# The first loads of an attention and spectral-mixing kernel: another queue for w_phi, another place for one weight load

## The chip, the cores and the metric

The kernel runs on one core of one Trainium2 chip. The metric is device time in microseconds (us), the median of the runs; the kernel before has 440.7 us in three runs (440.68 to 441.16). A core has five engines with an instruction stream each: TensorE (PE, matrix products; PEld is its loading of weights), VectorE (DVE), ScalarE (ACT), GpSimd (POOL) and SyncE (SP). Loads and stores are issued from one of these streams and carried out by 16 DMA engines that all issuers share. In the profile q0 is the DMA queue of what GpSimd issues, and q1 holds what SyncE issues.

## What is computed

The reference is an attention with a feature map, followed by a mixing of frequencies and channels:

```python
def phi(x):
    proj = einsum('bhsd,df->bhsf', x, w_phi)
    proj = proj - max(abs(proj), axis=-1)
    return concatenate([exp(proj), exp(-proj)], axis=-1)
q_p, k_p = phi(q), phi(k)
kv, z = einsum('bhsf,bhsd->bhfd', k_p, v), sum(k_p, axis=2)
x = einsum('bhsf,bhfd->bhsd', q_p, kv) / (einsum('bhsf,bhf->bhs', q_p, z) + 1e-6)
# heads side by side: x is (8, 576, 512)
X = rfft(x, axis=1)
Y[:, :64] = (Xr w_r - Xi w_i) + 1j (Xr w_i + Xi w_r)      # one matrix per mode
u = x + irfft(Y)
out = u + maximum(u @ w_ch, 0)
```

q, k and v are (8, 8, 576, 64) in float32, w_phi is 64 x 128. w_r and w_i are 64 matrices of 512 x 512 each, 134 MB together in float32, by far the most of what is read.

## The kernel before

The attention is cut into 16 units (class Unit, L101): a unit is two heads (g, 0 to 3) by two batches (bp, 0 to 3). Each unit loads its part of k and q as bfloat16 (load_k L105, load_q L109; the load converts) and of v as float32 (load_v L113). Each of these is one DMA with 2 x 128 rows of 2304 bytes on the reading side. The loop at L503 runs the units as a pipeline: in step n, one unit has its k and q turned by TensorE (turn_k, turn_q), the next earlier one gets its features and exponentials (rows_k, exp_k, rows_q), and the one before has its kv product, numerator and transform (weigh_v2, kv, num, freq). weigh_v2 multiplies v into va; that is the first use of a unit's v.

The weights w_r and w_i come in 64 loads of 1 MB as they land (2 MB as they are read), eight modes of 128 channels each; wload (L340) issues one, always on GpSimd, which converts float32 to bfloat16. next_w(n) (L359) issues the next n in the fixed list wq. The first of them, (0, 0), lands in the space of yacc (home, L327), the second in that of XT. Nine buffers of a pool and a few lent spaces hold the weights; mix (L461) uses them up, in the loop of the units through some (L488), and after it in the loop at L923, together with the second part: product with w_ch, inverse transform, relu, stores (Channels, Absorb, Last).

Each engine runs its instructions in the order of the program (class InOrder, L27): a helper records every instruction, and so the profile gives most of them the line L37. The tiles' names tell them apart. An instruction that waits for a semaphore holds up all that stands behind it in its engine's stream, the issues of DMAs among it.

The change is in the prologue, L365 to L386. There SyncE issues v of the first unit, w_phi twice (once for each half of the partitions, into scr, a space lent by xs) and v of the second unit (L368 to L371). GpSimd issues k and q of the first unit (L372, L373), then computes index tables with five kinds of iota (si, pi, nine, mi, L374 to L383) and the identity matrix (make_identity, L385), and then issues the first weights (next_w(1), L386); k and q of the second unit and another weight load come at L497 to L499. ScalarE begins with the loading of its function table for the sine, and then computes the sine (csf, L420). VectorE turns si and mi into angles (L400 to L419), casts the identity to ident_b (L421), which TensorE needs for every transpose, and casts w_phi into the two blocks of w2blk (L423, L424), which the first products of rows_k need.

Of the kernel before, what the change touches and what calls it, by code (L numbers as in the profile page):

```python
# [43 lines left out]
def kernel(  # L44
# [14 lines left out]
    pe, dve, act = (InOrder(tc, e) for e in (nc.tensor, nc.vector, nc.scalar))  # L59
    pool, sp = InOrder(tc, nc.gpsimd), InOrder(tc, nc.sync)  # L60
# [279 lines left out]
    def wload(g, w):  # L340
        wt = home(g, w)
        o, i = w // 2, w % 2
        w = (moe_w_r, moe_w_i)[i]
        pool.dma_start(
            wt.rearrange("p m r e -> p m (r e)"),
            w[MG * o:MG * o + MG, g * 128:(g + 1) * 128, :].rearrange(
                "m (p r) e -> p m (r e)", r=2))
        return wt
# [10 lines left out]
    def next_w(n):  # L359
        for _ in range(n):  # L360
            if wq:
                key = wq.pop(0)
                wts[key] = wload(*key)

    scr = xs[:, 1].rearrange("p b n d -> p (b n d)").bitcast(F32)  # L365
    wpf = scr[:, 1920:2048]
    units = [Unit(g, bp) for g in range(NG) for bp in range(NP)]
    units[0].load_v(sp)  # L368
    sp.dma_start(wpf[0:64, :], w_phi)
    sp.dma_start(wpf[64:128, :], w_phi)  # L370
    units[1].load_v(sp)  # L371
    units[0].load_k()  # L372
    units[0].load_q()  # L373
    si = const.tile([128, 5], I32, name="si")  # L374
    pool.iota(si[0:64, 0:4], [[1, 4]], base=0, channel_multiplier=9)
    pool.iota(si[0:64, 4:5], [[1, 1]], base=8, channel_multiplier=9)
# [6 lines left out]
    pool.iota(mi, [[4, 2], [8, NO], [1, 4]], base=0, channel_multiplier=0)  # L383
    ident_f = scr[:, 2176:2304]
    make_identity(nc, ident_f)  # L385
    next_w(1)  # L386

    w2blk = const.tile([128, 256], BF16, name="w2blk")
    wchb = const.tile([128, 4, 512], BF16, name="wchb")
# [664 lines left out]
```

## Time and profile before

| | before |
|---|---|
| median of 3 runs (lowest to highest) | 440.7 us (440.68 to 441.16) |
| span of the profiled execution, first to last instruction | 440.0 us |
| mean granted clock of TensorE | 0.909 |
| TensorE, matrix products busy | 326.7 us (74%) |
| VectorE busy | 296.0 us (67%) |
| ScalarE busy | 279.1 us (63%) |
| GpSimd busy | 112.5 us (26%) |
| read from HBM, written to it | 163.64 MB, 9.44 MB |

The profile is of one execution, whose time from end to end is not among the three runs; what it gives is the span, 0.7 us under their median. A busy time is the sum over the span and says nothing of where an engine was late. The page has the span in 40 slices of 11 us with the busy tenths of each engine and of the DMA engines, then the DMA queues with their share of 16 engines, then the chain of work that ended last, and the costliest groups of instructions with the idle time ahead of them. The trace behind it can be asked for one stretch of time: which instruction began when, what it waited for, and how many packets and bytes each queue moved. The DMA share can go over 1, since packets of one engine overlap. MB and GB/s of the page count the bytes that land.

### The profile page before, as it was taken

The page shows a single profiled execution, that of the slowest core. Times are in us where ns is not written, and L with a number is a line of the kernel's source. Part 1 is how long each engine was busy: PE and PEld are TensorE (multiplying, and loading weights), DVE is VectorE, ACT ScalarE, POOL GpSimd, SP SyncE. Part 2 cuts the span into 40 slices and gives each one's busy share as a digit, 9 for nine tenths or more (in the row PEclk, how much of TensorE's full clock was granted, in tenths as well). Part 3 has the DMA queues.
Part 4 walks back from the last instruction along what each step waited for, and adds up shares of the span by engine and source line. Part 5 has one row for each costly group of instructions (what it writes and reads, how often), then busy time and mean ns, then how long its engine had stood idle before and what let it go on. Part 6 is the DMA issues. An engine that isn't in the chain of part 4 may idle for free.

```text
span 440.0 us, 10106 instructions
## 1 busy us (share of the span) xinstructions
PE 326.7 (74%) x4190; PEld 199.7 (45%) x4233; DVE 296.0 (67%) x583; ACT 279.1 (63%) x478; POOL 112.5 (26%) x151
## 2 busy tenths in 40 slices
PE   1676668787678687778787777174679998997993
PEld 0445546555455455455455455051435454333320
DVE  5568787567785777886886878243883334885684
ACT  2788887687896777885875876210644442764782
POOL 6232132132211222221222121121101121582072
PEclk9989988689998799896896999675999999999997
DMA  8999999999999999999999999999999999996787
GB/s 193 210 211 210 237 212 238 231 217 241 235 211 239 221 230 234 237 213 235 228 221 238 210 235 209 236 209 212 212 215 223 220 221 223 206 218 150 238 361 310
DMA packets 51710, 99.55 MB, mean 226 GB/s; under 512 B 2512, under 2 KB 13648, under 8 KB 51664
## 3 DMA queue, kind: packets, MB, share of 16 engines
q0 software_dynamic: 45232, 85.86, 99.6%
q1 hardware_dynamic: 6432, 13.04, 8.5%
q8 instruction: 33, 0.54, 0.4%
q14 instruction: 13, 0.11, 0.1%
HBM read 163.64 MB, written 9.44 MB: 393 GB/s over the span
## 4 chain that ended last, share of the span: by engine, by line
PE 32%; DMA 31%; DVE 15%; ACT 15%; issue 5%; POOL 0%; POOLq 0%; ACTq 0%; DVEq 0%
DMA wt<-in_moe_w_i_dram 14%; PE pt L37 13%; PE one L37 12%; DMA wt<-in_moe_w_r_dram 8%; DMA vn<-in_v_dram 7%; ACT AB L37 6%; PE two L37 6%; DVE m L37 4%; DVE mk L37 4%; ACT AQ L37 3%; DMA qb<-in_q_dram 2%; PE pp L37 2%; ACT XT L37 2%; ACT qT L37 2%; DVE xw L37 1%
## 5 line engine op out<-in xcount | busy, mean ns | idle before, releaser
L37 ACT ACTIVATE AB<-two 128x1024 bf16<-128x1024 f32 x64 | 62.1, 1026 | 12.5 <-DVE mk L37 10.1
L37 ACT ACTIVATE AQ<-two 128x1024 bf16<-128x1024 f32 x64 | 62.7, 1046 | 1.3 <-PE two L37 1.2
L37 ACT CAST xw<-pt 128x512 bf16<-128x512 f32 x50 | 29.3, 587 | 42.3 <-PE pt L37 42.2
L37 DVE TENSOR_TENSOR va<-vn,ee 128x1152 bf16<-128x1152 f32 x32 | 42.0, 1355 | 11.9 <-DMA vn<-in_v_dram 11.9
L37 DVE TENSOR_REDUCE m<-two 128x8 f32<-128x1024 f32 x32 | 39.1, 1223 | 14.9 <-PE two L37 14.6
L37 DVE TENSOR_REDUCE mk<-two 128x8 f32<-128x1024 f32 x32 | 38.9, 1218 | 9.8 <-PE two L37 9.8
L37 POOL DMA_DIRECT2D wt<-in_moe_w_i_dram x28 | 20.9, 748 | 88.0 <-PE pt L37 36.2
L37 POOL DMA_DIRECT2D wt<-in_moe_w_r_dram x30 | 22.5, 749 | 72.3 <-PE one L37 29.3
L37 PE MATMUL pt<-wchb,xT 128*128 128x512 bf16 x127 | 34.7, 385 | 5.7 <-DVE xT L37 4.2
L37 PEld LDWEIGHTS <-xs 128*128 128x128 bf16 x624 | 31.3, 102 | 12.5 <-issue 7.5
L37 PE MATMUL two<-w2blk,qT 128*128 128x256 bf16 x128 | 21.9, 298 | 19.7 <-ACT AB L37 8.8
L37 ACT COPY qT<-one 128x512 bf16<-128x512 bf16 (+1 forms) x32 | 19.2, 641 | 26.4 <-PE one L37 26.2
L37 PE MATMUL one<-wt,XT 128*32 128x512 bf16 x304 | 27.7, 456 | 5.7 <-DMA wt<-in_moe_w_i_dram 4.1
L37 PE MATMUL one<-va,AB 64*128 64x65 bf16 x1024 | 23.1, 200 | 10.9 <-DVE va L37 10.9
L37 PEld LDWEIGHTS <-qT 128*128 128x128 bf16 x144 | 14.4, 102 | 36.7 <-issue 33.3
L37 PE MATMUL two<-mT,minus 96*128 96x512 bf16 x64 | 27.0, 423 | 3.4 <-issue 1.3
L37 DVE COPY xT<-pt 128x512 bf16<-128x512 bf16 x36 | 17.0, 472 | 17.3 <-PE pt L37 17.3
L37 PEld LDWEIGHTS <-AQ 128*128 128x128 bf16 x512 | 24.5, 108 | 8.2 <-issue 4.7
L37 PEld LDWEIGHTS <-XT 128*32 128x32 bf16 x512 | 14.7, 149 | 29.5 <-issue 23.2
L37 PE MATMUL one<-kvz,AQ 128*128 128x65 bf16 x512 | 27.2, 208 | 1.1 <-ACT qT L37 0.8
L37 DVE TENSOR_TENSOR xs<-one,rd 128x384 bf16<-128x384 f32 x48 | 26.8, 557 | 1.6
L37 PEld LDWEIGHTS <-AB 64*128 64x128 bf16 x1024 | 20.7, 101 | 15.0 <-DVE va L37 9.3
(151 smaller groups left out, 700.5 us busy)
## 6 DMA issues: line engine op xcount, KB each, us to landing
wt<-in_moe_w_r_dram POOLq DMA_DIRECT2D x30, 1024.0 KB, 28.6
wt<-in_moe_w_i_dram POOLq DMA_DIRECT2D x28, 1024.0 KB, 29.1
out_dram<-of SPq DMA_DIRECT2D x16, 512.0 KB, 3.7
vn<-in_v_dram POOLq DMA_DIRECT2D x14, 576.0 KB, 25.0
kb<-in_k_dram POOLq DMA_DIRECT2D x16, 288.0 KB, 22.0
qb<-in_q_dram POOLq DMA_DIRECT2D x16, 288.0 KB, 20.5
xs<-in_moe_w_i_dram POOLq DMA_DIRECT2D x2, 1024.0 KB, 24.1
vn<-in_v_dram SPq DMA_DIRECT2D x2, 576.0 KB, 6.7
```

What stands on the lines that cost most here:

```text
L37: ins = f(*args, **kwargs)
```

## The change

w_phi's two loads are issued on ScalarE's queue and not on SyncE's, so that in SyncE's stream v of the second unit follows v of the first directly. The first weight load moves up in GpSimd's stream, from behind the iotas and the identity to directly behind the first unit's q.

```diff
     units = [Unit(g, bp) for g in range(NG) for bp in range(NP)]
     units[0].load_v(sp)
-    sp.dma_start(wpf[0:64, :], w_phi)
-    sp.dma_start(wpf[64:128, :], w_phi)
+    act.dma_start(wpf[0:64, :], w_phi)
+    act.dma_start(wpf[64:128, :], w_phi)
     units[1].load_v(sp)
     units[0].load_k()
     units[0].load_q()
+    next_w(1)
     si = const.tile([128, 5], I32, name="si")
     pool.iota(si[0:64, 0:4], [[1, 4]], base=0, channel_multiplier=9)
...
     ident_f = scr[:, 2176:2304]
     make_identity(nc, ident_f)
-    next_w(1)
```

In the streams that come out of it, TensorE's and VectorE's are as before. ScalarE's has the two issues ahead of its first table load. GpSimd's has the same instructions, with the issue of the first weights ahead of the iotas; the order of the loads among themselves is as before. SyncE's begins with the two loads of v.

## The prediction

> **What bounds the kernel now.** I read the page from its bottom line of wide numbers inwards: the DMA row of the slices, the queues, the chain that ended last, and then the two places where the chain hangs on a load.
>
> On the page, the DMA row and the queues:
>
> ```profile
> DMA  8999999999999999999999999999999999996787
> ...
> q0 software_dynamic: 45232, 85.86, 99.6%
> q1 hardware_dynamic: 6432, 13.04, 8.5%
> ```
>
> q0 is the queue of GpSimd's loads. It is in use for 99.6% of the span; only the first slice (0 to 11 us) and the last four are below 9. The chain of waits, in order of time, near its end:
>
> ```profile
> 369.69 34.91 DMA wt<-in_moe_w_i_dram
> 404.65 0.69 PE pt L37 x8
> ```
>
> The last weights land at 404.6 us, 34.9 us after their issue: they spent that time behind other loads. What follows takes 440.0 - 404.6 = 35.4 us. TensorE's rows in the timeline, with the idle time in brackets, show the same before:
>
> ```profile
> 298.82 1.08 PE L37 MATMUL one<-wt,XT 128*32 128x512 bf16 x8 [4.11 <-DMA wt<-in_moe_w_i_dram]
> ...
> 303.81 1.08 PE L37 MATMUL pt<-wt,XT 128*32 128x512 bf16 x8 [3.91 <-DMA wt<-in_moe_w_r_dram]
> ...
> 404.65 0.66 PE L37 MATMUL pt<-wt,XT 128*32 128x512 bf16 x8 [0.94 <-DMA wt<-in_moe_w_i_dram]
> ```
>
> TensorE stood waiting for weights by 4.11 and 3.91 us near 300 us, and at the last weights by 0.94. So the end is set by the stream of loads: if the whole stream runs X earlier, TensorE leaves 303.8 us X earlier (X is less than both waits), meets the last weights X earlier and ends X earlier. The start of the calculation has slack instead: at 200 to 290 us VectorE's product va stood 9.9 us for v, by the waits of that stretch.
>
> What can the change do to a stream whose order it leaves alone? The loads on q0 come in the same order in both programs. So only the stretch in which the DMA engines moved less than they can is open. The stages, by the windows view (the last two columns are DMA share and GB/s landed):
>
> ```profile
> 2.50:4.00 1.50, 0.00 (x0) 0.00 (x0) 0.20 (x1) 0.00 (x0) 1.32 (x8) 1.00 0.92 336
> 4.00:7.00 3.00, 0.00 (x0) 0.00 (x0) 2.79 (x6) 0.00 (x0) 2.92 (x7) 1.00 0.98 143
> 7.00:10.00 3.00, 1.07 (x9) 0.88 (x9) 2.61 (x15) 1.16 (x2) 0.50 (x1) 1.00 1.13 287
> ```
>
> GB/s counts what is written; a load of k, q or weights reads float32 and writes bfloat16, so its reading is twice that. The queues of 4 to 7 us, then of 12 to 20 us (packets, MB, share):
>
> ```profile
> q0 software_dynamic: 326, 0.36, 86.2%
> q1 hardware_dynamic: 141, 0.07, 11.7%
> ```
>
> ```profile
> q0 software_dynamic: 1090, 1.68, 115.2%
> ```
>
> From 12 to 20 us, 2 x 1.68 = 3.36 MB are read in 8 us: 420 GB/s. From 4 to 7 us it is 2 x 0.36 + 0.07 = 0.79 MB in 3 us: 263 GB/s. Missing are 3 x 0.420 - 0.79 = 0.47 MB, at 420 GB/s **1.1 us of the stream**. From 2.5 to 4 us (0.50 MB on q1) another 0.13 MB, 0.3 us. From 7 to 10 us (0.33 MB on q0, 0.53 on q1) 1.19 MB, 397 GB/s, the hole is closed. So the hole is 1.1 + 0.3 = 1.4 us at most.
>
> Why is it there? The start in the timeline:
>
> ```profile
> 0.74 0.45 SPq L37 DMA_DIRECT2D vn<-in_v_dram  x1
> ...
> 1.25 1.24 SPq L37 DMA_DIRECT2D xs<-in_w_phi_dram  x2
> 1.28 0.86 POOL L37 DMA_DIRECT2D kb<-in_k_dram  x1 [0.83 <-POOLq L1038]
> ...
> 2.53 0.59 SPq L37 DMA_DIRECT2D vn<-in_v_dram  x1
> ```
>
> In the packet records, the first v (256 packets of 2304 bytes) runs from 1.8 to 4.1 us, w_phi's 128 packets of 512 bytes straggle from 3.7 to 6.9, and the second v, issued at 2.53, has its first packet at 6.67. k's first packet is at 4.0. In 4 to 7 us the engines thus have only q0 and a trickle of w_phi, while 0.59 MB of v stand behind the trickle.
>
> **The change, part by part.**
>
> *w_phi leaves SyncE's queue.* SyncE loses two issues, 1.24 us: the second v is issued at about 1.3 instead of 2.53 us, right behind the first, with nothing ahead of it in its queue. Its 0.59 MB then run in the hole: 0.47 + 0.13 = 0.60 MB were missing. Bounds: at best the hole closes, -1.4 us. At worst the hole is q0's own, because the first packets of a queue are slow: then v alternates with k and nothing is gained, 0. Some of it is: one of k's first packets took 1528 ns against a usual 107, and the eleven over 300 ns up to 7 us add up to some 6 us above the usual on single engines, 0.4 us on each of 16; I also take off 0.2 us because packets of a transfer are tied to their engines, which do not all have the hole. I take 1.4 - 0.4 - 0.2 = **-0.8 us**.
>
> A rule speaks against this: the Trainium skill, "DMA: Bandwidth & Descriptors", section "Issuing engines are not separate DMA queues", says that DMAs issued from several engines share the same 16 DMA engines and that this saves issue time only. Here 143 GB/s in one window beside 287 in the next says that the order in a queue left these engines underused; by the rule alone the sum would be 0.
>
> *What k and q lose.* Both units' v now share the engines with the first k and q. TensorE starts on k at 8.93 and on q at 10.94 us. If all of the second v goes ahead, that is 16 packets per engine of 93 to 106 ns: +1.6 us at most. In before, v's packets already took turns with k and q from 6.7 to 11 us (7 to 10 us: 261 packets on q0, 238 on q1), so most of this is a shift inside the same total; at best q gains what the hole gives, -1.1 us. I take 0 for q. Of the end it costs nothing while the stream holds it: the cover are the 9.9 us of va and the 4.11 of TensorE. If that cover is gone it costs its whole length.
>
> *w_phi on ScalarE.* No row shows an issue on ScalarE; by SyncE's row two cost 1.24 us. They stand ahead of the 1.28 us table load at 0.74, which moves to about 2.0 to 3.3 us. Behind it is the sine, at 7.34 after 5.32 us of idle time: cost 0, with 4 us of cover. At worst the new queue adds time outside of the span, which no row shows; I bound it by those 1.24 us and take 0. w_phi lands sooner; its casts into w2blk (7.48 us) are needed by the first product at 12.16.
>
> *The first weights ahead of the iotas.* GpSimd's issue (0.77 us) moves from 4.46 to about 2.95 and the iotas and the identity's two steps, 1.5 us in all, slip by 0.77. The next loads (k at 5.23) stay where they are, since the same instructions stand before them. q0 has k and q ahead of the weights, whose first packet runs at 8.5 us, 3.3 us after the old issue ended: the earlier issue gains 0, at best the 1.5 us by which it moves, if the stream were waiting for issues, but the engines are full there (397 GB/s from 7 to 10 us). The iotas feed VectorE: its rows from 3.43 on slip by 0.77. ident_b is cast at 7.99 instead of 7.22 and done at 8.3; the first transpose waits for k until 8.93. Cover 0.6 us, and if k lands sooner, q is still the later one. The sine ends at 8.9 instead of 8.1, ahead of the copy kT at 9.57. w2blk is ready at 8.7, 3.4 us early. Cost 0, bound +0.77.
>
> **Sum.** -0.8 + 0 + 0 + 0 on the profiled execution: 440.0 becomes 439.2. The median of the runs, 440.7, is 0.7 above that span; on it the forecast is 440.7 - 0.8 = **439.9 us**.
>
> **Rivals.**
>
> *A, the forecast:* the stream gains 0.4 to 1.2 us: 439.5 to 440.3. For it: 1.4 us of hole and 0.59 MB that fit. Chance 0.55, of which 0.25 over 0.2% (0.88 us, about the least that can be told from no change here) and 0.30 within it.
>
> *B, nothing:* the hole belongs to q0's first packets, or what the stream gains is lost behind 404.6 us; 440.4 to 441.0. For it: the 1528 ns packet, and that the last wait is only 0.94 us. Against it: q0 reaches 1.15 of share later with the same packets. 0.18.
>
> *C, slower:* v takes turns from the first k and q. q lands 1.6 us later, at 12.5, and every step of the chain from there to 114 us, which is calculation without a load in it, moves by as much. It decides if GpSimd's loads, which wait for TensorE to free buffers (36.2 and 29.3 us in the costliest groups), set the stream's pace, that is if their 20 to 35 us from issue to landing are used up: 440.7 + 1.6 = 442.3 us, or 441.5 when half of it comes through. Against it: no stage from 20 to 400 us has a DMA share under 1.1. 0.17.
>
> *D, more:* the whole hole closes and the weights' earlier issue counts as well: 1.2 to 2 us, 438.7 to 439.5. 0.10.
>
> Faster 0.25 + 0.10 = 0.35, same 0.30 + 0.18 = 0.48, slower 0.17. The range 439.2 to 441.5 leaves out half of D's stretch (0.04) and most of C's (0.12).
>
> **What would show it.** In the profile after: the window of 4 to 7 us with q1 near 0.5 MB instead of 0.07 and the total read near 1.2 MB; the last weights at 403.8 instead of 404.6; TensorE's first rows at 8.9 and 10.9 us within half a us. Wrong: q0 no faster by 12 us than before (B), or q at over 12 us and the last weights later than 404.6 (C). If the last weights come earlier and the end does not, the tail ate it.

## The result and the profile after

| | before | after |
|---|---|---|
| median of 5 runs each, us | 441.1 (440.68 to 442.33) | 439.48 (438.85 to 440.25) |
| span of the profiled execution, us | 440.0 | 438.5 |
| TensorE busy, us | 326.7 | 332.0 |
| TensorE's idle time for the last weights, us | 0.94 | none shown |

The ratio is 0.9966 (95% interval 0.995 to 0.9982): 1.5 us faster, 0.8 to 2.2. The forecast was 439.9 with a range of 439.2 to 441.5; the time lies inside. That it lies so near to 439.9 is in part luck: the forecast started from 440.7, the median of three runs, and with two runs more before has 441.1. As a difference, 0.8 us were forecast and 1.5 came. By the ratio "faster by over 0.2%" came (the end of its interval is 0.18%), which had a chance of 0.35; "within 0.2%" had more, 0.48. The time of 439.48 stands on the border between A (439.5 to 440.3) and D (438.7 to 439.5).

The page of after, its DMA row and its queues (packets, MB landed, share of 16 engines):

```profile
DMA  9999999999999999999999999999999999996787
...
q0 software_dynamic: 45232, 85.86, 99.7%
q1 hardware_dynamic: 6272, 12.98, 8.5%
...
q10 hardware_dynamic: 160, 0.07, 0.1%
...
PE 43%; DVE 22%; ACT 18%; DMA 10%; issue 5%; POOL 0%; POOLq 0%; ACTq 0%; DVEq 0%
```

The first slice went from 8 to 9, all others are as they were. q10 is ScalarE's queue; it holds w_phi and nothing else. The last line is the chain that ended last, by engine: loads have 10% of it. The same line of before, then of the changed kernel in a second profile (e10):

```profile
PE 32%; DMA 31%; DVE 15%; ACT 15%; issue 5%; POOL 0%; POOLq 0%; ACTq 0%; DVEq 0%
```

```profile
PE 35%; DMA 34%; ACT 13%; DVE 12%; issue 4%; POOL 0%; POOLq 0%; ACTq 0%; DVEq 0%
```

The loads' share of the chain thus differs as much between two executions of one kernel as between before and after, and says nothing of the change. The start of after in the timeline:

```profile
0.74 1.20 ACTq L37 DMA_DIRECT2D xs<-in_w_phi_dram  x2
0.74 0.96 SPq L37 DMA_DIRECT2D vn<-in_v_dram  x2
...
1.96 1.28 ACT L37 ACT_TABLE_LOAD   x1 [1.96 <-issue]
...
2.86 0.78 POOL L37 DMA_DIRECT2D yacc<-in_moe_w_r_dram  x1
...
7.93 0.22 DVE L37 CAST ident_b<-xs 128x128 bf16<-128x128 f32 x1
...
8.30 1.14 PE L37 MATMUL one<-ident_b,kb 128*128 128x128 bf16 x9 [8.30 <-DVE nine L37]
...
9.69 1.28 PE L37 MATMUL one<-ident_b,qb 128*128 128x128 bf16 x10 [0.25 <-DMA qb<-in_q_dram]
```

Two issues on ScalarE take 1.20 us and the table load moves to 1.96, as the sum had it. TensorE begins with k at 8.30 and with q at 9.69 us, 0.6 and 1.25 us sooner than before. The first of these two ended a wait for VectorE: the cast of the identity (ident_b) had become as late as k. The hole of 4 to 7 us, by the windows view (last columns DMA share and GB/s) and by queue:

```profile
4.00:7.00 3.00, 0.00 (x0) 0.00 (x0) 2.27 (x6) 0.00 (x0) 2.84 (x9) 1.00 1.11 292
```

```profile
q1 hardware_dynamic: 271, 0.57, 52.3%
q0 software_dynamic: 224, 0.26, 52.0%
q10 hardware_dynamic: 126, 0.05, 6.7%
```

Read are 2 x 0.26 + 0.57 + 0.05 = 1.14 MB in place of 0.79. The second v now runs here. TensorE's rows at the places where it waited for weights:

```profile
297.11 0.66 PE L37 MATMUL one<-wt,XT 128*32 128x512 bf16 x8 [3.30 <-DMA wt<-in_moe_w_i_dram]
...
302.11 1.08 PE L37 MATMUL pt<-wt,XT 128*32 128x512 bf16 x8 [4.34 <-DMA wt<-in_moe_w_r_dram]
...
403.11 0.66 PE L37 MATMUL pt<-wt,XT 128*32 128x512 bf16 x8
```

The waits near 300 us are still there, so TensorE is still led by the stream up to 302 us, which it leaves 1.70 us sooner. At the last weights it shows no wait, and the last load in the chain is the one that ends at 302 us (start, length, both in us):

```profile
265.36 36.71 DMA wt<-in_moe_w_r_dram
```

From 302 us on it is calculation, on TensorE and VectorE above all, that sets the end of this execution. This too is no mark of the change: the granted clock from 305 to 437 us was 0.98 in before and 0.95 in after, and e1 and e3, which have the gain, wait 0.59 and 0.96 us there, as e2, which has no gain of the stream, waits 0.58.

### The profile page after: what moved, and what is told of

The parts are those of the page before. It is cut to its first block, busy times and chain, and to the rows that moved or that the text cites. A ratio compares the mean times of both kernels' runs of the same rounds, so it can differ in the third digit from the quotient of the medians.

```text
span 438.5 us, 10107 instructions
## 1 busy us (share of the span) xinstructions
PE 332.0 (76%) x4190; PEld 202.1 (46%) x4233; DVE 296.4 (68%) x583; ACT 279.4 (64%) x478; POOL 113.0 (26%) x151
## 4 chain that ended last, share of the span: by engine, by line
PE 43%; DVE 22%; ACT 18%; DMA 10%; issue 5%; POOL 0%; POOLq 0%; ACTq 0%; DVEq 0%
PE pt L37 17%; PE one L37 14%; DMA wt<-in_moe_w_r_dram 8%; PE two L37 8%; ACT AB L37 7%; DVE m L37 6%; DVE mk L37 6%; PE pp L37 4%; ACT AQ L37 3%; ACT XT L37 3%; DVE xs L37 2%; DVE XT L37 2%; DMA qb<-in_q_dram 2%; ACT qT L37 1%; DVE yacc L37 1%
## 5 line engine op out<-in xcount | busy, mean ns | idle before, releaser
L37 PE MATMUL pt<-wchb,xT 128*128 128x512 bf16 x127 | 35.6, 393 | 5.2 <-DVE xT L37 3.5
L37 PE MATMUL two<-mT,minus 96*128 96x512 bf16 x64 | 28.5, 446 | 3.2 <-issue 1.5
L37 PEld LDWEIGHTS <-AQ 128*128 128x128 bf16 x512 | 25.8, 111 | 8.8 <-issue 5.6
L37 PE MATMUL one<-kvz,AQ 128*128 128x65 bf16 x512 | 28.4, 212 | 1.2 <-ACT qT L37 0.8
L37 DVE RECIPROCAL rd<-one 128x6 f32<-128x6 f32 x48 | 9.4, 196 | 27.6 <-PE one L37 27.5
L37 POOL DMA_DIRECT2D kb<-in_k_dram x16 | 11.4, 714 | 62.2 <-PE one L37 57.2
```

Of the source, the lines that this page charges most:

```text
L37: ins = f(*args, **kwargs)
```

## The experiments

My theory: the stream of loads sets the end; the second v directly behind the first, in whatever queue w_phi goes, fills the hole and advances the whole stream. Rival 1: the weights' earlier issue counts. Rival 2: k and q land sooner, and the calculation starts sooner. Rival 3: a second hardware queue is what helps. In the table, "stream" is when the sixth megabyte had been read, against before's profile (18.16 us); a negative number is sooner. It is from the packet records; of k, q and the weights twice as much is read as lands. "k's first packet" is from the same records. One more thing that the runs with both v first have in common, the earlier landing of the second v (5.5 to 6.7 us instead of 11.6), is not what counts: in before VectorE first reads it at 41.83 us, without a wait.

| run | ratio to before (95%) | read 4 to 7 us, MB | stream, us | k's first packet, us | TensorE begins q, us |
|---|---|---|---|---|---|
| after | 0.9966 (0.995 to 0.9982) | 1.13 | -1.05 | 5.4 | 9.7 |
| e10, after again | 0.9958 (0.9944 to 0.9972) | 1.11 | -1.08 | 5.2 | 9.5 |
| e1, w_phi only | 0.9964 (0.9949 to 0.9978) | 1.19 | -1.21 | 5.4 | 9.1 |
| e3, w_phi last on SyncE | 0.9965 (0.9951 to 0.9978) | 1.19 | -0.96 | 5.1 | 9.0 |
| e5, v on both queues | 0.9961 (0.9947 to 0.9976) | 1.17 | -1.03 | 5.3 | 9.7 |
| e8, after with a late start | 0.9962 (0.9948 to 0.9977) | 1.08 | -0.93 | 5.5 | 11.8 |
| e9, k and q behind iotas | 0.9972 (0.9957 to 0.9987) | 1.16 | -1.00 | 5.4 | 9.9 |
| e7, w_phi first | 0.9985 (0.9975 to 0.9995) | 1.21 | -0.04 | 2.9 | 10.3 |
| e2, weights only | 0.9988 (0.9975 to 1.0002) | 0.89 | 0.00 | 4.0 | 10.7 |
| e6, second v on GpSimd | 0.9999 (0.9983 to 1.0016) | 0.89 | -0.36 | 4.0 | 9.2 |
| e4, both v behind q | 0.9997 (0.9979 to 1.0014) | 1.06 | +0.44 | 2.9 | 10.0 |
| before | 1 | 0.79 | 0 | 4.0 | 10.9 |

**e1, one part alone: w_phi on ScalarE.** The weights stay where they were.

```diff
-    sp.dma_start(wpf[0:64, :], w_phi)
-    sp.dma_start(wpf[64:128, :], w_phi)
+    act.dma_start(wpf[0:64, :], w_phi)
+    act.dma_start(wpf[64:128, :], w_phi)
     units[1].load_v(sp)
```

> Only w_phi moves to ScalarE's queue; the first weights stay behind the iotas. Theory (order of SyncE's queue: v behind v fills the hole of 4 to 7 us): all of the gain, time 0.996 to 0.997 of before; 4 to 7 us read near 1.1 MB; weights' first packets at 8.0 to 8.5 us as in after. Rival 1 (the weights' earlier issue gives a part): about half of it, 0.998, and the first weight packets later than in after. Rival 2 (nothing of the prologue, other chance): 1.000.

0.9964: all of the gain. The weights' first packet came at 8.3 us against 8.4 in after, with the issue 1.6 us later. The earlier issue, rival 1, is not needed for any of it.

**e2, the other part alone: the first weights ahead of the iotas.**

```diff
     units[0].load_q()
+    next_w(1)
...
     make_identity(nc, ident_f)
-    next_w(1)
```

> Only the first weights move ahead of the iotas; w_phi stays between the two loads of v on SyncE. Theory: nothing, 1.000 within 0.001, with the hole of 4 to 7 us as in before (0.8 MB read). Rival 1 (earlier issue counts): 0.997 to 0.998, 0.8 us or more.

The stream did not move (0.00 us at 6 MB, -0.05 at 100 MB), and the ratio's interval holds 1. The weights' first packet came 0.8 us sooner than in before (7.9 for 8.8 us), but the hole was still there, and at 6 MB nothing was left of it:

```profile
q0 software_dynamic: 366, 0.41, 98.5%
q1 hardware_dynamic: 147, 0.08, 10.5%
```

That is e2 from 4 to 7 us: 0.08 MB on q1, w_phi and the very beginning of v, as in before.

**e3, the order without the queue: SyncE issues v, v, w_phi.**

```diff
     units[0].load_v(sp)
+    units[1].load_v(sp)
     sp.dma_start(wpf[0:64, :], w_phi)
     sp.dma_start(wpf[64:128, :], w_phi)
-    units[1].load_v(sp)
```

> w_phi stays on SyncE's queue but behind both loads of v; weights as in before. Theory (the order in the queue): the same gain as with ScalarE's queue, 0.996 to 0.997; w_phi's last packets near 6 us, in time for its casts at 7.5. Rival 3 (a second hardware queue is what helps): 1.000, and the engines as poorly used from 4 to 7 us as in before.

0.9965, the same gain with one queue. w_phi's packets ran until 7.7 us and did not matter. It is the order in the queue that counts, not ScalarE's queue; rival 3 falls. That agrees with what the Trainium skill says of issuing engines ("DMA: Bandwidth & Descriptors", section "Issuing engines are not separate DMA queues"), that several of them save only the time of issuing. I had read it as speaking against the change, but the other queue was only a way to take w_phi out from between the two v.

**e4, when can q0 begin? Both v on GpSimd behind q, w_phi alone on SyncE.**

```diff
-    units[0].load_v(sp)
     sp.dma_start(wpf[0:64, :], w_phi)
     sp.dma_start(wpf[64:128, :], w_phi)
-    units[1].load_v(sp)
     units[0].load_k()
     units[0].load_q()
+    units[0].load_v()
+    units[1].load_v()
```

> Both loads of v on GpSimd behind k and q, w_phi alone on SyncE. It tells when q0 can begin: in before k's first packet was at 4.0 us, just as the first v ended, in after at 5.4, just as the second v ended. If q1's loads hold q0 back, k's first packet now comes well ahead of 4.0 (3 us or sooner) and q lands by about 7.5 us; if q0 begins at its own time, at 4.0 us, and the DMA engines are idle until then, some 0.9 MB are lost: 1.002 to 1.004 of before.

With nothing but w_phi on q1, k's first packet came at 2.9 us, from the same issue at 1.28. So in before (4.0 us) and in after (5.4) k had been held back by v. The Trainium skill ("DMA: Bandwidth & Descriptors", section "Queues, rings and completion order") says that each DMA engine changes between queues packet by packet, and that a packet there has 9 to 17 descriptors as a rule. A load of v is 256 of the profile's packets, 16 for each of the 16 engines. If each is one descriptor, k's start behind one v in before fits a turn of a whole load; its start behind two v in after does not, since 32 per engine went ahead. Why both went ahead is not shown. The price of the early beginning was an empty start: 0.44 us of the stream were lost. The time was that of before within its interval (-0.9 to +0.6 us), so this loss was too small to be seen in it. TensorE, held by the identity until 9.05 us, began q 0.9 us sooner than in before, and gained nothing by it.

**e5, both hardware queues at once, weights early as in after.**

```diff
     units[0].load_v(sp)
     sp.dma_start(wpf[0:64, :], w_phi)
     sp.dma_start(wpf[64:128, :], w_phi)
-    units[1].load_v(sp)
+    units[1].load_v(act)
```

> As after, but the second v is issued on ScalarE's queue and w_phi on SyncE's behind the first v, so that both v can run at once from about 2 us. In after and its relatives the single queue reads 364 to 415 GB/s from 3 to 5 us, under the 420 of later. Theory (the engines' rate before q0 begins is what is left to gain): 2 to 5 us at 400 or more, the stream another 0.2 to 0.4 us ahead at 12 us, time 0.995 to 0.9965 of before. Rival (one queue after the other already fills the engines): as after, 0.9965.

My expectation failed: the two v ran side by side from 2.5 us, each at about half, and 2.5 to 4 us landed 329 GB/s against 328 in after. Two queues at once brought nothing more; the time is that of after.

**e6, the second v taken out of the hole: on GpSimd behind q, w_phi on ScalarE.**

```diff
-    sp.dma_start(wpf[0:64, :], w_phi)
-    sp.dma_start(wpf[64:128, :], w_phi)
-    units[1].load_v(sp)
+    act.dma_start(wpf[0:64, :], w_phi)
+    act.dma_start(wpf[64:128, :], w_phi)
     units[0].load_k()
     units[0].load_q()
+    units[1].load_v()
```

> w_phi on ScalarE, first v on SyncE, second v on GpSimd behind q, weights as in before. So nothing but w_phi and k, q compete from 4 to 7 us, and q0 begins at 4.0 us as in before. If the hole of before came of the second v's and w_phi's turns between k and q, it closes: 1.1 MB or more read from 4 to 7 us, gain as after, 0.9965. If the hole is q0's own slow beginning at 4.0 us, it stays: 0.8 to 0.95 MB, time 0.998 to 1.000.

The queues of e6 from 4 to 7 us:

```profile
q0 software_dynamic: 383, 0.42, 100.2%
q10 hardware_dynamic: 100, 0.04, 5.0%
q1 hardware_dynamic: 7, 0.00, 0.5%
```

k and q alone, with w_phi out of the way by 4.9 us, read 2 x 0.42 + 0.04 = 0.88 MB: the hole stays, without the second v in any queue ahead of k or beside it. Seventeen packets of the first k and q took 280 to 1050 ns in place of 107. They add up to 7.1 us above the usual, 0.44 us on each of 16 engines, about half of what is missing from 4 to 7 us (3 x 0.42 - 0.89 = 0.37 MB, 0.9 us); the other half is not accounted for. What rival B of the prediction said, that the hole belongs to q0's first packets, is thus right at least in part. But the second v fills it all the same, as k waits until v is through, and its packets and q's are then fast: in e1, e3 and e10 none of them took over 280 ns. Of the 1.05 us of stream, e6 gets 0.36 without v in the hole; the other 0.7 come with it.

**e7, w_phi first on SyncE, then v and v.**

```diff
     units = [Unit(g, bp) for g in range(NG) for bp in range(NP)]
+    sp.dma_start(wpf[0:64, :], w_phi)
+    sp.dma_start(wpf[64:128, :], w_phi)
     units[0].load_v(sp)
-    sp.dma_start(wpf[0:64, :], w_phi)
-    sp.dma_start(wpf[64:128, :], w_phi)
     units[1].load_v(sp)
```

> SyncE issues w_phi, then v and v; weights as in before. Theory (v directly behind v): 0.9965 to 0.998, the first v's packets begin later by the 1.2 us of w_phi's issues, so up to 1.2 us of the start is lost again; the second v fills 4 to 7 us. Rival (w_phi must leave SyncE): 1.000.

0.9985, short of the 0.998 that I had as the worst. From 4 to 7 us 1.21 MB were read, the most of all, but the loss had moved ahead: k began at 2.9 us with slow packets, w_phi's packets straggled on q1 until 4.4 us, v began behind them at 4.9, and 2.5 to 4 us landed 63 GB/s. The stream at 6 MB was where before had it. v directly behind v was not enough; the gain came only in the runs in which nothing stood ahead of the two v in SyncE's and ScalarE's queues.

**e8, after with a late start.** Five copies of VectorE ahead of the sine, into a table that is overwritten.

```diff
+    for _ in range(5):
+        dve.tensor_copy(csf, ang)
     act.activation(csf, ang, ACT.Sin, scale=2.0 * math.pi / S_)
```

> after, with five copies more on VectorE ahead of the sine and the identity's cast (they write a table that is overwritten), so that the first transposes and q's come 2 to 3 us later; the loads of the prologue are as in after. Theory (the stream of loads sets the end, the start of the calculation has slack): as after, 0.996 to 0.997 of before, within 0.5 us of after. Rival (the gain is k and q landing sooner): the gain is gone and more, 1.001 to 1.003.

```profile
10.84 1.12 PE L37 MATMUL one<-ident_b,kb 128*128 128x128 bf16 x9 [10.84 <-DVE ident_b L37]
11.75 1.30 PE L37 MATMUL one<-ident_b,qb 128*128 128x128 bf16 x10
```

TensorE begins k 2.5 us and q 2.1 us later than in after, later even than in before, and the time is 0.9962. The start of the calculation has that much slack; rival 2 falls.

**e9, e1 with k and q issued behind the iotas.**

```diff
-    units[0].load_k()
-    units[0].load_q()
     si = const.tile([128, 5], I32, name="si")
...
     make_identity(nc, ident_f)
+    units[0].load_k()
+    units[0].load_q()
     next_w(1)
```

> As e1 (w_phi on ScalarE), but GpSimd issues k and q only behind the iotas and the identity, 1.6 us later, at 2.8 and 3.6 us; the two v run on q1 until 5.4 us as in e1. In the runs so far q0's first packets were slow (300 to 1500 ns instead of 107) where q0 began 1.4 to 2.7 us after the issue of k, and not where it began 4.1 us after it. If that lead is what counts (GpSimd's descriptors must be ahead of the engines), the slow packets come back from 5.4 us on, 4 to 8 us read 0.1 to 0.3 MB less than in e1, and the time is 0.9975 to 0.999. If it counts only that q1 is busy until then, as e1: 0.9965.

k was issued only 1.0 us later, at 2.31 us, and began at 5.4 as in e1. Six slow packets came back (370 to 830 ns) and the stream lost 0.2 us against e1, but 1.00 us is still within what the other runs with v first have (0.92 to 1.21), and 0.9972 lies between the two expectations, with an interval that holds both. Whether the lead counts, the time from the issue of k to its first packet (3.1 us here, 4.2 in e1), is not settled by this run; why q0's first packets are slow when it begins early stays open.

**e10, the changed kernel again, beside e9.**

> The changed kernel once more, beside e9 on one chip: 0.9965 of before, stream 1.0 to 1.2 us ahead of before at 12 us and at 240 us, in every execution with k's first packet near 5.4 us and q landed before 10 us.

0.9958, k's first packet at 5.2 us, TensorE on q at 9.5 us, the stream 1.08 us ahead at 6 MB and 1.15 at 100 MB (at 243 us): as expected.

## Why the prediction was right, and where it was not

- *What bounds the kernel.* Right, and tested: e8 starts the calculation 2 us later and loses nothing; e6 begins q 1.7 us sooner than before and gains nothing that its interval shows; all seven runs with the stream 0.9 to 1.2 us ahead at 6 MB are faster, by 0.28 to 0.42%, and the four with 0.36 us or less lie within 0.15% of before. What was too strict is that the end moves by just as much as the stream. Single executions do not follow that: e6, with 0.36 us of stream, left 302 us as early as after (302.12 and 302.11 us) and yet has the time of before, and from TensorE's leaving 302 us to the end the runs took between 135.6 and 137.5 us.
- *w_phi leaves SyncE's queue, -0.8 us.* The sign and the place were right (e1, e3), the size was short: the stream gained 1.05 us in after and 1.21 in e1, of a hole of 1.4. The term that was mis-sized is the 0.4 us for q0's slow packets. I took them to stay; with q0 beginning later they went from eleven to four in after (1.0 us above the usual, 0.06 per engine) and to none in e1. The 0.2 us for packets that are tied to their engines can't be checked, as the records don't name a packet's engine; the runs without any slow packet of k and q (e1, e3, e8, e10) left 0.2 to 0.5 us of the hole. The 143 beside 287 GB/s that I held against the rule of the skill are what landed; by what was read they are 263 beside 397.
- *k and q.* I had v take turns with them packet by packet, with 0 for q and TensorE's first rows within half a us. That step failed: both v went ahead of k, k's first packet moved from 4.0 to 5.4 us, and yet q was begun 1.25 us sooner, since q0 then runs at its full rate and q no longer meets the second v. As predicted, it counted for nothing at the end.
- *w_phi on ScalarE, 0.* Right. Time and span of the runs of after differ by 1.75 to 1.83 us, those of before by 1.73 to 1.86 in the runs that list both: the new queue costs nothing outside of the span.
- *The weights ahead of the iotas, 0.* Right for the stream (e2: 0.00). ident_b was cast at 7.93 (I had 7.99) and done at 8.15, but k landed sooner than I had it, and the cover of 0.6 us was gone: in after k landed at 8.28 us, level with the identity, and in e10 at 8.03, where TensorE then waited for the identity until 8.20. It cost nothing at the end, by e8. A gain of up to 0.25% in e2 can't be excluded by its interval.
- *The bridge from span to time.* The two differ by 1.8 us, not 0.7, so the profiled execution of before, at some 441.8 us, was a long one among its runs. So was that of after: 440.25 us, the longest of its five. The stream of before shows where its own was lost: at 130 MB it is 0.65 us behind e2 and e7, with which it was level at 100 MB (0.05 us). So of the 1.76 us between before and after at 130 MB, some 1.1 are of the change, and the 1.5 us between the two profiled spans must not be taken for its gain. The spans of all profiles agree: the seven runs with the gain average 438.3 us, e2, e4, e6 and e7 439.4. The 1.5 us of the ratio have an interval of 0.8 to 2.2 that holds the stream's 1.05; whether the rest is more than scatter was not settled: e7, with the stream where before had it, is at 0.9985 and its interval leaves out 1, while e4 and e6 are at 1.
- *The tail.* The sign that I named, the last weights at 403.8 instead of 404.6, came and more: TensorE took them at 403.11, and their last packet ended at 401.9 us, in before at 404.1. The last wait of 0.94 us is gone in after, but in e1 and e3 it is not, so rival B's loss behind the last weights is not shown by these runs.
- *What is left.* e5, the one try at more, does not differ from after; of the 1.4 us of hole 0.2 to 0.5 are left in the runs with both v first.

## What to carry to other kernels

Where a queue of loads is never empty, look for the one stretch in which the engines moved less than elsewhere, and count it in bytes: what can be put there moves the whole stream, and with it the end (here about 1 us of stream and 0.3 to 0.4% of the time; 0.4 us of stream either way could not be seen in the time). A load that is needed late can be the right one to run first, if the queue that matters is slow to begin. Here the small load belonged behind the large ones in an issuing engine's queue (e3), not between them (before) and not ahead of them (e7). A later start of the calculation by 2 us cost nothing (e8), since the stream decided.

## What the runs showed of the hardware that was not expected

Loads of v under way on q1 held q0's first load back: with the same issue of k at 1.28 us its first packet came at 4.0 us behind one v, whose last packet began at 4.0 too, and at 5.1 to 5.5 behind two. w_phi did not: k's first packet came at 2.9 us in the midst of w_phi's (2.1 to 3.5 us in e4, to 4.4 in e7). And the second v of before did not hold back q, which was under way: from 7 to 10 us q0 and q1 had 261 and 238 packets. Second, how slow q0's first packets are went with when it began: from 2.9 or 4.0 us, nine to seventeen packets of k and q took 280 to 1530 ns; from 5.1 us or later, none to four with k issued at 1.28 us, and six with it issued at 2.31. Why is not shown for either.
